# Value and feed-forward loads issued from the ScalarE queue instead of the SyncE queue, in a one-core attention decode kernel

## The chip, the cores and the metric

The kernel runs on one core of a Trainium2 chip. The metric is device time in microseconds (us). The kernel before takes 692.99 us (median of 4 runs, 691.93 to 693.73). A run counts as slow when it is over 1.5% above the fastest run of the same kernel.

In this text K5 is the key load of head 5, V5 its value load, wo1 the second load of output weights (each serves four heads). "Ring" is the line of packets that one issuing engine's loads form at the DMA engines (in the profiles q1 for SyncE, q10 for ScalarE). A "slot" is one half of the double buffer that holds keys or values. "PV" is the product of the softmax probabilities and the values, "fold" the sum of a position's 128 products of key and query.

## The reference, cut to what matters

One token of a transformer block: a layer norm modulated by a condition vector, attention over a cache of 16384 positions in 32 heads of 128, then a gated feed-forward layer.

```python
    B, Sq, D = (1, 1, 640)
    Hq, Hkv, Sk, Dh = (32, 32, 16384, 128)          # bf16 caches: 4 MB of keys and 4 MB of values a head
    ...
    scores = jnp.einsum('bhqd,bhkd->bhqk', q, k) * Dh ** (-0.5)
    p = _softmax(scores, axis=-1)
    o = jnp.einsum('bhqk,bhkd->bhqd', p, v)
    ...
    h = _layernorm(x, axis=-1) * (1 + ca) + sa
    x = x + ga * _A_ref(h, A_k_cache, A_v_cache, A_wq, A_wo)
    h = _layernorm(x, axis=-1) * (1 + cb) + sb
    x = x + gb * _B_ref(h, B_w_gate, B_w_up, B_w_down)
```

There is one query per head, so every byte of the caches is used once: 290 MB have to come in, nearly all of it keys and values.

## The kernel before

The program is a list of operations, each with an engine, a position and the operations that it waits for. Each engine runs its own in order of position; a DMA belongs to the engine that issues it, and that engine stands still until the DMA's waits are met and its issue is done: in the kernel before SyncE waits 556.4 us in all for the first folds that free key slots.

```python
        def lead(h):
            return 1 if h < H - 8 else 2          # keys run ahead of values by 1 head, by 2 in the last 8 heads
        ...
        order = []                                # order of the loads on SyncE's queue
        for h in range(H):
            while nk < min(H, h + lead(h) + 1):
                order.append(("k", nk)); nk += 1  # (two lines joined here)
            if h % G == 0:                        # G = 4
                order.append(("wo", h // G))
            order.append(("v", h))
        ...
            d_k[h] = plan.dma(qpos["k", h], kring[:, s2], ..., deps=[o_fold1[h - 2]] if h >= 2 else [])
            d_wo[g] = plan.dma(qpos["wo", g], woring[:, g % 2],
                               A_wo[...].rearrange("(g p) n -> p g n", p=128), ...)   # rows of 1280 bytes
            vdeps = [o_pvlast[h - 2]] if h >= 2 else [o_mod_a, o_mod_b]
            d_v[h] = [plan.dma(qpos["v", h] + 0.01 * c, vring[...], ..., deps=vdeps) ...]
        ...
            o_mult[h]  = op(DVE,  ..., deps=[d_k[h], o_qbc[h]])          # keys times query
            o_fold1[h] = op(DVE,  ..., deps=[o_mult[h], ...])            # first half of the sum; frees the key slot
            o_fold[h]  = op(PE,   ..., deps=[o_fold1[h], ...])           # rest of the sum
            o_red[h]   = op(DVE,  ...)
            o_max[h]   = op(DVE,  ...)
            o_gm[h]    = op(POOL, ..., deps=[o_max[h]])                  # maximum over partitions
            o_nb[h]    = op(ACT,  ..., deps=[o_gm[h]])
            o_exp[h]   = op(ACT,  ..., deps=[o_nb[h], ...])
            o_pvlast[h] = op(PE,  ..., deps=[o_exp[h], d_v[h][0], ...])  # PV; frees the value slot
        ...
        # after the last head, on SyncE's queue: w_gate, w_up, w_down (three loads, rows of 1280 bytes)
```

(Cuts are marked with dots. The comments are added here.) On PE, PV of head h stands ahead of the fold of head h+1 (of h+2 in the last eight heads), so the heads form one chain.

## Time and profile before

| | before |
|---|---|
| span of the profiled execution | 690.0 us |
| DMA, mean over the span | 422 GB/s |
| one key or value load: 8 packets of 32 KB on each of 16 engines, 1.21 us a packet | 9.7 us |
| multiply of head 0, 25, 30, 31 starts at | 38.1, 526.4, 621.7, 640.0 us |
| from the multiply of head 31 to the end | 50.0 us |

The page's 40 slices of the span (busy tenths of the 16 DMA engines, then GB/s) and its table of DMA queues (packets, MB, time of the packets as a share of 16 engines' span), kernel before:

```profile
DMA  9999999999999999999999999999999999999995
GB/s 385 422 423 435 434 427 428 427 431 429 430 419 433 434 431 434 420 438 426 430 433 425 432 429 428 427 428 429 437 432 421 434 432 427 425 433 424 400 425 202
...
q1 hardware_dynamic: 16368, 290.48, 98.8%
```

Nine tenths or more in all slices but the last, and all of it on queue q1, SyncE's. The DMA engines have no room: q1's packets alone take 98.8% of their time. The chain of waits followed back from the last instruction, by engine and then by line, kernel before:

```profile
DMA 40%; DVE 21%; PE 18%; POOL 18%; ACT 2%; issue 1%; SPq 1%
DMA kring<-in_A_k_cache_dram 36%; POOL gm L417 18%; DVE kring L397 13%; PE psb L407 9%; PE psb L436 7%; DVE f L399 6%; DMA kring<-in_B_w_down_dram 4%; DVE S_sb L411 2%; ACT P_sb L421 1%; PE psb L470 1%; DVE pm L414 1%; SPq L71 1%; PE psb L523 0%; PE psb L388 0%; ACT nb L419 0%
```

Keys are what is waited for most (36%), but over half of the chain is computation: POOL's maximum, the multiply, PE's fold and PV. Two of the groups of instructions (busy us, mean ns; then idle time before them and its cause):

```profile
L397 DVE TENSOR_TENSOR kring<-kring,qbc_sb 128x16384 bf16<-128x16384 bf16 x32 | 278.0, 8687 | 30.2 <-DMA kring<-in_A_k_cache_dram 28.5
L417 POOL PARTITION_ALL_REDUCE gm<-pm x32 | 136.7, 4272 | 333.5 <-DVE pm L414 327.5
```

The maximum takes 0.35 us by itself and 8.73 us when the next head's multiply (8.69 us) has started just ahead of it; 4.27 is a mean of the two kinds. In this execution 15 of the 32 maxima start 0.17 to 0.18 us after a multiply and take 8.71 to 8.73 us; the 17 others start while no multiply runs and take 0.35. Whether a head's maximum or the next head's multiply starts first is a race that decides 8 us.

The same kernel's timeline in time order (start us, duration us, engine), the first loads of values and the first multiply:

```profile
21.37 0.34 SPq L71 DMA_DIRECT2D vring<-in_A_v_cache_dram  x1
...
38.08 8.69 DVE L397 TENSOR_TENSOR kring<-kring,qbc_sb 128x16384 bf16<-128x16384 bf16 x1 [13.97 <-DMA kring<-in_A_k_cache_dram]
...
51.26 0.33 SPq L71 DMA_DIRECT2D kring<-in_A_k_cache_dram  x1
...
51.62 0.43 SPq L71 DMA_DIRECT2D vring<-in_A_v_cache_dram  x1
```

V0 waits for the modulation weights, which lie in its slot, and has K0, K1 and wo0 ahead of it in the ring; K2 and V1 come at 51.

Two stretches of the view by windows (us; busy us and count of PE, weight loads, DVE, ACT, POOL; PE clock; DMA share; GB/s):

```profile
70.00:78.00 8.00, 6.03 (x40) 2.84 (x32) 3.43 (x4) 1.00 (x3) 2.61 (x2) 0.88 1.02 436
78.00:84.00 6.00, 0.00 (x0) 0.00 (x0) 6.00 (x1) 0.00 (x0) 6.00 (x1) 0.56 1.00 431
...
576.00:584.00 8.00, 7.76 (x48) 3.38 (x40) 2.46 (x4) 1.00 (x3) 1.75 (x1) 0.72 1.04 446
584.00:600.00 16.00, 6.20 (x49) 2.52 (x50) 13.04 (x3) 2.42 (x9) 12.36 (x2) 0.68 0.99 426
```

And the end of the timeline, last two multiplies, then the last head's maximum and the first ScalarE step after it:

```profile
621.69 8.68 DVE L397 TENSOR_TENSOR kring<-kring,qbc_sb 128x16384 bf16<-128x16384 bf16 x1
...
639.97 8.68 DVE L397 TENSOR_TENSOR kring<-kring,qbc_sb 128x16384 bf16<-128x16384 bf16 x1
...
659.35 0.35 POOL L417 PARTITION_ALL_REDUCE gm<-pm  x1 [6.00 <-DVE psb L499]
659.74 0.20 ACT L419 ACTIVATE nb<-gm 128x1 f32<-128x1 f32 x1 [5.37 <-POOL gm L417]
```

ScalarE starts 0.04 us after the maximum has ended.

### The profile page before, as it was taken

Reading aid. Unit: us, or ns where it says so; the run is one execution under the profiler, and the core shown is the slowest. Engines: PE = TensorE matmul, PEld = TensorE weight load, DVE = VectorE, ACT = ScalarE, POOL = GpSimd, SP = SyncE. Lnnn points to the kernel's source line nnn. Section 1 sums busy time; section 2 is a strip of 40 time slices with the busy share of each in tenths; the row PEclk is TensorE's granted clock in tenths of the full one; section 3 lists DMA queues with packets and bytes.
Section 4 is the critical chain, followed back from the end, with each engine's and each line's share of the span. In section 5 each row is a group of like instructions: output and inputs, shape, how many; then the busy total and the mean of one; then the engine's idle time right before and its main releaser. Section 6 shows DMA issues by size and latency. Waiting matters only on the chain.

```text
span 690.0 us, 5939 instructions
## 1 busy us (share of the span) xinstructions
PE 305.9 (44%) x2602; PEld 150.5 (22%) x2602; DVE 453.8 (66%) x151; ACT 80.1 (12%) x306; POOL 280.4 (41%) x75
## 2 busy tenths in 40 slices
PE   1503454545444334455432455444335345454464
PEld 1401122222212122222111222212112122221144
DVE  0077767676778876657787566668766676767800
ACT  0100101111111111110111111101011011111110
POOL 0006666565677554000405033304054365667700
PEclk9997666666767666666766666657666666767675
DMA  9999999999999999999999999999999999999995
GB/s 385 422 423 435 434 427 428 427 431 429 430 419 433 434 431 434 420 438 426 430 433 425 432 429 428 427 428 429 437 432 421 434 432 427 425 433 424 400 425 202
DMA packets 16398, 290.86 MB, mean 422 GB/s; under 512 B 1458, under 2 KB 7284, under 8 KB 7284
## 3 DMA queue, kind: packets, MB, share of 16 engines
q1 hardware_dynamic: 16368, 290.48, 98.8%
q8 instruction: 20, 0.33, 0.2%
q14 instruction: 6, 0.05, 0.0%
q10 hardware_dynamic: 4, 0.00, 0.0%
HBM read 290.47 MB, written 0.00 MB: 421 GB/s over the span
## 4 chain that ended last, share of the span: by engine, by line
DMA 40%; DVE 21%; PE 18%; POOL 18%; ACT 2%; issue 1%; SPq 1%
DMA kring<-in_A_k_cache_dram 36%; POOL gm L417 18%; DVE kring L397 13%; PE psb L407 9%; PE psb L436 7%; DVE f L399 6%; DMA kring<-in_B_w_down_dram 4%; DVE S_sb L411 2%; ACT P_sb L421 1%; PE psb L470 1%; DVE pm L414 1%; SPq L71 1%; PE psb L523 0%; PE psb L388 0%; ACT nb L419 0%
## 5 line engine op out<-in xcount | busy, mean ns | idle before, releaser
L397 DVE TENSOR_TENSOR kring<-kring,qbc_sb 128x16384 bf16<-128x16384 bf16 x32 | 278.0, 8687 | 30.2 <-DMA kring<-in_A_k_cache_dram 28.5
L417 POOL PARTITION_ALL_REDUCE gm<-pm x32 | 136.7, 4272 | 333.5 <-DVE pm L414 327.5
L436 PE MATMUL psb<-vring,P_sb 128*32 128x512 bf16 x992 | 108.6, 616 | 138.3 <-DMA vring<-in_A_v_cache_dram 138.3
L424 POOL PARTITION_ALL_REDUCE Ls<-rs x32 | 140.7, 4396 | 27.3 <-ACT P_sb L421 27.3
L407 PE MATMUL psb<-f,ident 128*128 128x512 bf16 x512 | 135.0, 421 | 27.9 <-DVE f L399 27.9
L399 DVE TENSOR_TENSOR f<-kring 128x8192 bf16<-128x8192 bf16 x32 | 141.6, 4425 | 1.1
L411 DVE TENSOR_REDUCE S_sb<-psb 128x128 f32<-128x512 f32 x32 | 22.1, 692 | 153.2 <-PE psb L407 153.2
L470 PE MATMUL psb<-On,woring 128*128 128x1 bf16 x160 | 11.6, 182 | 160.7 <-ACT On L462 159.7
L407 PEld LDWEIGHTS psb<-f,ident 128*128 128x128 bf16 x512 | 50.7, 104 | 120.5 <-DVE f L399 49.5
L436 PEld LDWEIGHTS psb<-vring,P_sb 128*32 128x32 bf16 x992 | 33.5, 138 | 190.8 <-DMA vring<-in_A_v_cache_dram 140.4
L470 PEld LDWEIGHTS psb<-On,woring 128*128 128x128 bf16 x160 | 8.9, 130 | 162.3 <-ACT On L462 162.3
L419 ACT ACTIVATE nb<-gm 128x1 f32<-128x1 f32 x32 | 6.5, 203 | 307.6 <-POOL gm L417 307.6
L447 PEld LDWEIGHTS psb<-sel,acc_sb 128*128 128x128 f32 x248 | 32.3, 191 | 5.8 <-ACT acc_sb L441 1.2
L441 ACT ACTIVATE acc_sb<-psb 128x512 f32<-128x512 f32 x31 | 18.5, 597 | 117.9 <-PE psb L436 117.8
L447 PE MATMUL psb<-sel,acc_sb 128*128 128x1 f32 x248 | 29.4, 240 | 0.7 <-ACT acc_sb L441 0.7
L426 ACT ACTIVATE lnl<-Ls 128x1 f32<-128x1 f32 x32 | 6.4, 201 | 115.8 <-POOL Ls L424 115.8
L388 PE MATMUL psb<-R_sb,ones_bf 128*128 128x128 bf16 x32 | 8.3, 259 | 23.6 <-ACT R_sb L385 23.6
L421 ACT ACTIVATE P_sb<-S_sb,nb 128x128 bf16<-128x128 f32 x32 | 12.8, 401 | 1.0
L385 ACT ACTIVATE R_sb<-ident,q_r 128x128 bf16<-128x128 bf16 x32 | 12.5, 389 | 0.0
L391 ACT ACTIVATE qbc_sb<-psb 128x128 bf16<-128x128 f32 x32 | 8.9, 277 | 11.2 <-PE psb L388 11.2
L414 DVE TENSOR_REDUCE pm<-S_sb 128x1 f32<-128x128 f32 x32 | 9.2, 286 | 1.1
L308 POOL PARTITION_ALL_REDUCE st<-st x2 | 0.8, 391 | 20.8 <-DVE x L488 11.2
(62 smaller groups left out, 80.3 us busy)
## 6 DMA issues: line engine op xcount, KB each, us to landing
kring<-in_A_k_cache_dram SPq DMA_DIRECT2D x32, 4096.0 KB, 25.6
vring<-in_A_v_cache_dram SPq DMA_DIRECT2D x31, 4096.0 KB, 34.4
wreg<-in_A_wq_dram SPq DMA_DIRECT2D x1, 5120.0 KB, 27.1
woring<-in_A_wo_dram SPq DMA_DIRECT2D x8, 640.0 KB, 25.5
vring<-in_w_mod_dram SPq DMA_DIRECT2D x1, 4800.0 KB, 14.3
vring<-in_A_v_cache_dram SPq DMA_DIRECT2D x4, 1024.0 KB, 9.7
wreg<-in_B_w_gate_dram SPq DMA_DIRECT2D x1, 2160.0 KB, 16.7
wreg<-in_B_w_up_dram SPq DMA_DIRECT2D x1, 2160.0 KB, 21.6
```

The costliest lines, as they stand in the source:

```text
L397: o_mult[h] = op(DVE, base, lambda e, kslot=kslot, qb=qb: e.tensor_tensor(out=kslot, in0=kslot, in1=qb, op=ALU.mult), deps=[d_k[h], o_qbc[ ...
L399: o_fold1[h] = op(DVE, base + 8.8, lambda e, kslot=kslot: e.tensor_tensor(out=f1[:], in0=kslot[:, :, 0:64], in1=kslot[:, :, 64:128], op=AL ...
L407: r = e.matmul(S_ps[s2][:].rearrange("p (t r) -> p t r", r=GC), lhsT=ident[:], rhs=f1[:, :, GC * m:GC * (m + 1)], start=(m == 0), stop=(m ...
L411: o_red[h] = op(DVE, base + 17.0, lambda e, s2=s2: e.tensor_reduce(out=S_sb[:, s2], in_=S_ps[s2][:].rearrange("p (t r) -> p t r", r=GC), a ...
L414: o_max[h] = op(DVE, base + 19.3, lambda e, h=h, s2=s2: e.tensor_reduce(out=pm[:, h:h + 1], in_=S_sb[:, s2], axis=AX.X, op=ALU.max), deps= ...
L417: o_gm[h] = op(POOL, base + 19.6, lambda e, h=h: e.partition_all_reduce(gm[:, h:h + 1], pm[:, h:h + 1], channels=128, reduce_op=bass.bass_ ...
L421: o_exp[h] = op(ACT, base + 20.4, lambda e, h=h, s2=s2, sp=sp: e.activation(out=P_sb[:, sp, 0:TT], in_=S_sb[:, s2], func=ACTF.Exp, scale=S ...
L424: o_L[h] = op(POOL, base + 21.0, lambda e, h=h: e.partition_all_reduce(Ls[:, h:h + 1], rs[:, h:h + 1], channels=128, reduce_op=bass.bass_i ...
L436: r = e.matmul(acc_ps[s2][q4:q4 + 32, :], lhsT=P_sb[:, sp, 4 * j:4 * j + 32], rhs=vring[:, s2, 4 * j:4 * j + 4, :].rearrange("p a d -> p ( ...
L441: o_acc[h] = op(ACT, vbase + 9.0, lambda e, s2=s2: e.activation(out=acc_sb[:, s2, :], in_=acc_ps[s2][:], func=ACTF.Copy), deps=[o_pvlast[h ...
L447: r = e.matmul(OT_ps[:, h:h + 1], lhsT=acc_sb[:, s2, 128 * i:128 * (i + 1)], rhs=sel[:, i:i + 1], start=(i == 0), stop=(i == 3))
L470: r = e.matmul(attn_ps[:, cc:cc + 1], lhsT=wv[:, cc, :], rhs=On[:, h:h + 1], start=(h == 0 and cc == 0), stop=(h == H - 1 and cc == KC - 1 ...
```

## The change

Its intent: put values on a second queue, so that a value load need not stand behind a key load whose slot is still in use, and the other way round. Keys and output weights stay on SyncE.

```diff
+        def vpos(h):
+            if h < 2:
+                return 1.97
+            return T0 + (h - 2) * PERIOD + 10.5 + PERIOD * lead(h - 2) + 9.2
 ...
-            d_v[h] = [plan.dma(qpos["v", h] + 0.01 * c, vring[...], ...
-                               ("v", s2) if nvp == 1 else ("vp", s2, c), deps=vdeps, name=...) for c in range(nvp)]
+            d_v[h] = [plan.dma(vpos(h) + 0.01 * c, vring[...], ...
+                               ("v", s2) if nvp == 1 else ("vp", s2, c), deps=vdeps, eng="act", name=...) for c in range(nvp)]
 ...
+        QA = vpos(H - 1) + 0.1
-        d_wg = plan.dma(QE, wg_v, ..., "wg", deps=[o_qmm], name="dma_wg")
+        d_wg = plan.dma(QA, wg_v, ..., "wg", deps=[o_qmm], eng="act", name="dma_wg")
 ... # w_up and the three w_down loads in the same way, behind it
```

More of the change, by code (lines that the diff above doesn't have):

```diff
@@ L381, in build @@
             vdeps = [o_pvlast[h - 2]] if h >= 2 else [o_mod_a, o_mod_b]
-            d_v[h] = [plan.dma(qpos["v", h] + 0.01 * c, vring[:, s2, c * VP:(c + 1) * VP, :], kv(A_v, h)[:, c * VP:(c + 1) * VP, :],
-                               ("v", s2) if nvp == 1 else ("vp", s2, c), deps=vdeps, name="dma_v%d_%d" % (h, c)) for c in range(nvp)]
+            d_v[h] = [plan.dma(vpos(h) + 0.01 * c, vring[:, s2, c * VP:(c + 1) * VP, :], kv(A_v, h)[:, c * VP:(c + 1) * VP, :],
+                               ("v", s2) if nvp == 1 else ("vp", s2, c), deps=vdeps, eng="act", name="dma_v%d_%d" % (h, c)) for c in range(nvp)]
             o_R[h] = op(ACT, base - 15.0 if h > 0 else 2.5, lambda e, h=h, s2=s2: e.activation(
@@ L476, in build @@
         QE = float(len(order)) + 1.0
-        d_wg = plan.dma(QE, wg_v, B_wg.rearrange("(p k) n -> p k n", k=KC), "wg", deps=[o_qmm], name="dma_wg")
-        d_wu = plan.dma(QE + 0.01, wu_v, B_wu.rearrange("(p k) n -> p k n", k=KC), "wu", deps=[o_qmm], name="dma_wu")
+        QA = vpos(H - 1) + 0.1
+        d_wg = plan.dma(QA, wg_v, B_wg.rearrange("(p k) n -> p k n", k=KC), "wg", deps=[o_qmm], eng="act", name="dma_wg")
+        d_wu = plan.dma(QA + 0.01, wu_v, B_wu.rearrange("(p k) n -> p k n", k=KC), "wu", deps=[o_qmm], eng="act", name="dma_wu")
         wd_src = B_wd[0:128 * FJ, :].rearrange("(j p) n -> p j n", p=128)
         NJA = FJ - 3
-        d_wd = [plan.dma(QE + 0.02, wd_v[:, 0:NJA], wd_src[:, 0:NJA], "wd0", deps=[o_fold1[H - 2]], name="dma_wd0"),
-                plan.dma(QE + 0.03, wdr_v[0:FR], B_wd[128 * FJ:F, :], "wdr", deps=[o_fold1[H - 2]], name="dma_wdr"),
-                plan.dma(QE + 0.04, wd_v[:, NJA:FJ], wd_src[:, NJA:FJ], "wd1", deps=[o_fold1[H - 2]], name="dma_wd1")]
+        d_wd = [plan.dma(QA + 0.02, wd_v[:, 0:NJA], wd_src[:, 0:NJA], "wd0", deps=[o_fold1[H - 2]], eng="act", name="dma_wd0"),
+                plan.dma(QA + 0.03, wdr_v[0:FR], B_wd[128 * FJ:F, :], "wdr", deps=[o_fold1[H - 2]], eng="act", name="dma_wdr"),
+                plan.dma(QA + 0.04, wd_v[:, NJA:FJ], wd_src[:, NJA:FJ], "wd1", deps=[o_fold1[H - 2]], eng="act", name="dma_wd1")]
         o_abf = op(ACT, TE, lambda e: e.activation(out=attn_bf[:], in_=attn_ps[:, 0:KC], func=ACTF.Copy), deps=[o_wo[H - 1]], name="attn_bf")
```

## The prediction

(Two sentences are cut from it, about the maximum beside the multiply and about how two rings are served: they told of the hardware what no trace had shown. No term of the sum is cut: 6 + 14 - 3 = 17, with up to 4 for a late K31, taken as 18. That the rings share evenly and bring no bandwidth, on which terms 1 and 2 rest, was the author's assumption at that point; what the traces then showed is in point 1 of "Why the prediction was wrong".)

> **What bounds the kernel now.** The page shows the 16 DMA engines 9 tenths busy or more in all 40 slices but the last, 422 GB/s on average. In the packet records a 32 KB packet takes 1.21 us, so a 4 MB key or value load (8 packets per engine) costs 9.7 us. 64 of them are 623 us; with the weights the engines have about 680 us of work in a span of 690. Issue time is no limit: 0.33 us a load, which lands 25.6 us (keys) or 34.4 us (values) later. What can change is the order in which bytes arrive, and the gaps.
>
> A second limit is close. In the chain of waits, heads 0 to 9 and 25 to 31 run on computation: multiply 8.7, fold 4.4, PE fold 4 to 5, reductions 1.0; the maximum on GpSimd takes 8.73 us when the next head's multiply runs (else 0.35); then exp, PV 3.5. From the multiply of head 25 (526.4) to that of 31 (640.0) a head takes 18.9 us, and the end comes 50 us later, 3 of them waits for feed-forward loads. [...]
>
> **What the change does.** 35 value and 5 feed-forward loads leave SyncE's ring for ScalarE's. ScalarE issues each in about 0.35 us, off the chain. [...] No bandwidth comes, but the keys lose their place:
>
> 1. Start. V0 and V1 issue at about 23.5 us (today V1: 51.6). They share with wq, K0 and K1: K0 lands near 49.5 instead of 38. All slots are full and K2 is loaded by 78; the next slot comes free when fold 1 of head 1 ends, near 82.5. The engines idle about 6 us.
> 2. Middle. Values run as far ahead as their two slots allow. When K25 lands, about 25.5 value loads have gone before it instead of 24: 14 us. Output weights (1280-byte packets, 55 ns) alternate with 32 KB value packets and hold back the keys behind them.
> 3. Heads 24 to 31. Value loads wait on ScalarE behind the next head's exp; the engines idle some 4 and 2 us. The loop of 18.9 us runs on from a K25 about 20 us late.
> 4. End. The feed-forward loads land before they are needed: about 3 us come back.
>
> Sum: 6 + 14 - 3 = 17, with up to 4 for a late K31: 693 + 18.
>
> **Predicted: 711 us**, 8 in 10 between 701 and 720. Faster by over 2%: 0.02; within 2%: 0.27; slower by over 2%: 0.71.
>
> **What would show it.** First multiply near 50 us (now 38.1); a DMA gap of some 6 us near 80; multiply of head 25 near 546; value loads landing about 20 us after issue; the chain in the last 150 us on computation, without a wait for w_down; about 432 GB/s wherever the DMA isn't idle.
>
> **What would make it wrong.** If the rings don't share evenly (keys first), steps 1 and 2 shrink and the time stays near 693. If two rings fill the engines better than one, it is within 2%. If small packets starve the keys longer, it is above 720.

## More of the kernel before

The view of the line that issues all DMAs (count; shortest, median and longest issue in ns; first and last start), kernel before:

```profile
L71 SPq DMA_DIRECT2D vring<-in_A_v_cache_dram x35: 327/432/1386, 21.4 to 655.1; - x35
...
L71 SPq DMA_DIRECT2D kring<-in_B_w_down_dram x3: 438/2161/15974, 657.1 to 659.8; - x3
```

A value load issues in 0.43 us. One of the w_down loads took 16 us to issue; on SyncE only the store of the result stands behind it, issued at 686.82 us, 11 us after this issue has ended (675.79).

## The result, and the profile after

The changed kernel took 726.53 us (720.12 to 735.83, 4 runs); the ratio to the kernel before is 1.045 (95% interval 1.039 to 1.052). In a second round it took 722.78 us (718.75 to 726.24), 1.044. Ratios are the mean time of one kernel's fast runs over that of the other's of the same rounds, so not quite the ratio of the medians quoted. The loss is 31 to 34 us where 18 was predicted, and the time spreads over 2% from run to run where the kernel before spreads over 0.3%.

The seven executions that are not slow lie within 1.1% (718.75 to 726.54). The first profiled execution was the 735.83 us one, slow. So I read a profile of the second round (722.6 us, span 720.6). Its line numbers are a few higher than before (the multiply is L397 before and L402 after). Slices and queues:

```profile
DMA  9999699999999999999999999999999969999980
GB/s 380 433 431 422 246 437 434 423 429 435 433 383 420 432 435 430 425 429 433 433 397 430 425 435 430 425 430 433 433 416 427 400 281 435 425 428 435 414 319 2
...
q1 hardware_dynamic: 9264, 149.62, 49.2%
q10 hardware_dynamic: 7108, 140.86, 45.7%
```

The work is now halved between q1 (keys) and q10 (ScalarE's), and it has holes: at slices 5, 33 and the last two. Not a slower rate: in the packet records a 32 KB packet's median is 1.21 us in both kernels, on both rings, and between the holes GB/s is what it was. The chain:

```profile
DMA 30%; DVE 25%; PE 22%; POOL 16%; ACTq 3%; ACT 2%; issue 1%; SPq 0%; POOLq 0%; DVEq 0%
DMA kring<-in_A_k_cache_dram 30%; POOL gm L422 16%; DVE kring L402 14%; PE psb L412 12%; DVE f L404 7%; PE psb L441 7%; ACTq L71 3%; DVE S_sb L416 2%; ACT P_sb L426 1%; PE psb L475 1%; PE psb L512 1%; DVE pm L419 1%; PE psb L462 1%; PE psb L529 0%; ACT nb L424 0%
```

A new entry is ACTq, ScalarE's queue issuing DMAs, with 3%. The groups:

```profile
L422 POOL PARTITION_ALL_REDUCE gm<-pm x32 | 220.7, 6897 | 324.0 <-DVE pm L419 300.3
L402 DVE TENSOR_TENSOR kring<-kring,qbc_sb 128x16384 bf16<-128x16384 bf16 x32 | 277.9, 8684 | 51.8 <-DMA kring<-in_A_k_cache_dram 51.8
```

The multiply waits 51.8 us for keys where it waited 30.2, and more maxima lose the race (mean 6.9 us). The start:

```profile
24.50 0.36 ACTq L71 DMA_DIRECT2D vring<-in_A_v_cache_dram  x1
24.90 0.45 ACTq L71 DMA_DIRECT2D vring<-in_A_v_cache_dram  x1
...
49.18 8.69 DVE L402 TENSOR_TENSOR kring<-kring,qbc_sb 128x16384 bf16<-128x16384 bf16 x1 [23.68 <-DMA kring<-in_A_k_cache_dram]
```

V0 and V1 go out at 24.5 us and share the engines with K0: the first multiply moves from 38.1 to 49.2. The windows:

```profile
70.00:78.00 8.00, 0.00 (x0) 0.00 (x0) 8.00 (x1) 0.00 (x0) 8.00 (x1) 0.55 0.82 352
78.00:84.00 6.00, 4.51 (x35) 1.46 (x36) 4.57 (x2) 2.27 (x8) 4.00 (x2) 0.50 0.29 79
...
576.00:584.00 8.00, 5.54 (x40) 1.94 (x41) 5.56 (x2) 2.27 (x8) 4.99 (x2) 0.57 0.27 72
584.00:600.00 16.00, 5.96 (x48) 3.12 (x50) 13.74 (x4) 1.41 (x6) 11.86 (x2) 0.68 0.99 426
```

Against 431 and 446 GB/s before, the engines do little in 78 to 84 and 576 to 584 us. The issues and the end of the timeline:

```profile
L71 ACTq DMA_DIRECT2D vring<-in_A_v_cache_dram x35: 334/334/453, 24.5 to 669.5; - x35
...
L71 ACTq DMA_DIRECT2D kring<-in_B_w_down_dram x3: 457/600/21472, 670.9 to 692.9; - x3
...
L71 ACTq DMA_DIRECT2D wreg<-in_B_w_up_dram x1: 453/453/453, 670.5 to 670.5; - x1
```

```profile
644.55 8.68 DVE L402 TENSOR_TENSOR kring<-kring,qbc_sb 128x16384 bf16<-128x16384 bf16 x1
...
668.67 8.69 DVE L402 TENSOR_TENSOR kring<-kring,qbc_sb 128x16384 bf16<-128x16384 bf16 x1 [5.75 <-DMA kring<-in_A_k_cache_dram]
...
670.95 22.60 ACTq L71 DMA_DIRECT2D kring<-in_B_w_down_dram  x3
...
688.31 0.35 POOL L422 PARTITION_ALL_REDUCE gm<-pm  x1 [23.71 <-DVE psb L505]
693.59 0.20 ACT L424 ACTIVATE nb<-gm 128x1 f32<-128x1 f32 x1 [24.83 <-issue]
```

The view by DMA issues tells the w_down loads apart (KB, us from issue to landing):

```profile
kring<-in_B_w_down_dram ACTq DMA_DIRECT2D x1, 1600.0 KB, 29.2
...
kring<-in_B_w_down_dram ACTq DMA_DIRECT2D x1, 80.0 KB, 29.0
```

Value loads issue in 0.33 us. But one w_down load takes 21.5 us to issue, now on ScalarE. It is the second of the three, the 80 KB one (64 rows, issued at 671.44); the large one ahead of it (1280 rows, 670.95) issues in 0.46 us. And the last head's first ScalarE step (nb) starts 4.9 us after its maximum has ended (688.66), when the issues are over (670.95 + 22.60 = 693.55): the idle time before it is put down to "issue". K31's multiply comes 24.1 us after that of head 30 (18.3 before), and from it to the end are 51.9 us.

Sums over the packet records of the two traces, in bins of 1 us: the DMA engines are idle for 10.2 us of the span before and 38.6 after, and busy for 679.8 and 682.1. The 30.6 us of longer span are in these two differences. The idle time is 1.9 us at the very start (2.0 before), 6.9 near 80, 2.3 in the middle, 6.5 near 580, and 20.9 at the end (7.4 at the end before).

### The profile page after: what moved, and what is told of

The parts are those of the page before. It is cut to its first block, busy times and chain, and to the rows that moved or that the text cites. A ratio compares the mean times of both kernels' runs of the same rounds, so it can differ in the third digit from the quotient of the medians.

```text
span 733.9 us, 5939 instructions
## 1 busy us (share of the span) xinstructions
PE 315.9 (43%) x2602; PEld 153.4 (21%) x2602; DVE 453.3 (62%) x151; ACT 79.2 (11%) x306; POOL 305.6 (42%) x75
## 3 DMA queue, kind: packets, MB, share of 16 engines
q1 hardware_dynamic: 9264, 149.62, 48.3%
## 4 chain that ended last, share of the span: by engine, by line
DMA 33%; DVE 28%; PE 21%; POOL 14%; ACT 2%; issue 1%; SPq 0%; POOLq 0%; DVEq 0%
DMA kring<-in_A_k_cache_dram 33%; DVE kring L402 17%; POOL gm L422 14%; PE psb L412 13%; DVE f L404 8%; PE psb L441 6%; DVE S_sb L416 2%; ACT P_sb L426 1%; PE psb L475 1%; PE psb L512 1%; DVE pm L419 1%; PE psb L462 1%; PE psb L529 0%; PE psb L393 0%; ACT nb L424 0%
## 5 line engine op out<-in xcount | busy, mean ns | idle before, releaser
L422 POOL PARTITION_ALL_REDUCE gm<-pm x32 | 178.5, 5579 | 356.1 <-DVE pm L419 329.2
L402 DVE TENSOR_TENSOR kring<-kring,qbc_sb 128x16384 bf16<-128x16384 bf16 x32 | 277.9, 8685 | 66.2 <-DMA kring<-in_A_k_cache_dram 64.8
L412 PE MATMUL psb<-f,ident 128*128 128x512 bf16 x512 | 151.9, 460 | 161.8 <-DVE f L404 161.8
L429 POOL PARTITION_ALL_REDUCE Ls<-rs x32 | 124.0, 3875 | 27.3 <-ACT P_sb L426 27.3
L412 PEld LDWEIGHTS psb<-f,ident 128*128 128x128 bf16 x512 | 54.7, 112 | 265.3 <-DVE f L404 184.0
L441 PE MATMUL psb<-vring,P_sb 128*32 128x512 bf16 x992 | 101.7, 584 | 0.0
L446 ACT ACTIVATE acc_sb<-psb 128x512 f32<-128x512 f32 x31 | 18.3, 590 | 15.9 <-PE psb L441 15.8
L298 PE MATMUL psb<-silu_c,vring 128*128 128x1 bf16 x150 | 6.2, 178 | 7.1 <-DMA vring<-in_w_mod_dram 7.1
```

What stands on the lines that cost most here:

```text
L402: o_mult[h] = op(DVE, base, lambda e, kslot=kslot, qb=qb: e.tensor_tensor(out=kslot, in0=kslot, in1=qb, op=ALU.mult), deps=[d_k[h], o_qbc[ ...
L412: r = e.matmul(S_ps[s2][:].rearrange("p (t r) -> p t r", r=GC), lhsT=ident[:], rhs=f1[:, :, GC * m:GC * (m + 1)], start=(m == 0), stop=(m ...
L422: o_gm[h] = op(POOL, base + 19.6, lambda e, h=h: e.partition_all_reduce(gm[:, h:h + 1], pm[:, h:h + 1], channels=128, reduce_op=bass.bass_ ...
L429: o_L[h] = op(POOL, base + 21.0, lambda e, h=h: e.partition_all_reduce(Ls[:, h:h + 1], rs[:, h:h + 1], channels=128, reduce_op=bass.bass_i ...
L441: r = e.matmul(acc_ps[s2][q4:q4 + 32, :], lhsT=P_sb[:, sp, 4 * j:4 * j + 32], rhs=vring[:, s2, 4 * j:4 * j + 4, :].rearrange("p a d -> p ( ...
L446: o_acc[h] = op(ACT, vbase + 9.0, lambda e, s2=s2: e.activation(out=acc_sb[:, s2, :], in_=acc_ps[s2][:], func=ACTF.Copy), deps=[o_pvlast[h ...
```

## The experiments

All have correct results unless a wrong one is said to be on purpose. Those based on the changed kernel start with a, those on the kernel before with b. "Idle" is the DMA engines' idle time in the profiled execution, read as above (its last figure is that of the last 30 us of the span); "m31" is the start of the last multiply.

| run | median us | ratio to before | first multiply | idle at the start, middle, near 545 to 590, end | head 30 to 31 | m31 to end |
|---|---|---|---|---|---|---|
| before | 693.0 | 1 | 38.1 | 0, 0, 0, 7.4 | 18.3 | 50.0 |
| after_again | 722.8 | 1.044 | 49.2 | 6.9, 2.3, 6.5, 20.9 | 24.1 | 51.9 |
| a_wo_pool | 718.7 | 1.039 | 47.7 | 5.6, 0, 6.8, 20.0 | 19.4 | 57.6 |
| a_no_wo (wrong result) | 712.0 | 1.029 | 47.3 | 4.1, 0.3, 7.0, 20.3 | 18.8 | 57.9 |
| a_wd_sp | 726.3 | 1.049 | 47.7 | 4.1, 6.1, 6.5, 19.0 | 29.7 | 45.3 |
| a_wo_pool_wd_sp | 709.4 | 1.025 | 47.4 | 4.6, 0, 6.3, 11.7 | 19.9 | 47.7 |
| c1_first_two | 704.7 | 1.016 | 37.7 | 0, 0.7, 7.0, 12.2 | 19.8 | 48.3 |
| c2_lead_one | 702.1 | 1.014 | 38.1 | 0, 0.4, 0, 18.0 | 19.2 | 43.6 |
| a_mid_only | 709.2 | 1.025 | 37.8 | 0, 11.7, 8.7, 7.2 | 19.3 | 49.2 |
| a_tail_sp | 715.2 | 1.031 | 47.6 | 5.1, 5.5, 8.0, 7.2 | 18.3 | 49.3 |
| a_tail_only | 712.1 | 1.028 | 38.0 | 0, 0, 8.0, 18.9 | 29.7 | 45.4 |
| a_v01_sp | 718.5 | 1.035 | 38.3 | 0, 8.8, 5.8, 19.2 | 29.7 | 45.5 |

(Gaps of up to 3.3 us in other places are left out. The last digits of the idle times and of the middle columns are those of one execution each; the runs of one kernel spread by some us.)

### Output weights: the same kernel again, without them beside the keys, without them at all

My theory: besides the value loads it is the output weights that hold back the keys. They consist of 32 packets of 1280 bytes per engine; a packet takes 55 ns, but beside a value load on the other ring they wait for value packets of 1.21 us. In the packet records of the repeated profile (us from the span's start, first packet to end of the last of each load):

```
K5   122.9 to 141.7
wo1  142.3 to 155.5     1.8 us of packets, stretched to 13.2 (3.8 in the kernel before)
V5   143.0 to 154.3
K6   153.8 to 168.4     K6 stands behind wo1: 27 us after K5
```

From 144.5 to 152.5, 97 packets of wo1 start and 97 of V5: one for one. In the first profiled execution (the slow one) the five output-weight loads with 84 to 131 value packets beside them take 12.4 to 13.6 us from first to last packet, the three with at most 16 take 3.4 to 3.9; on the one ring of the kernel before all eight take 3.8 to 5.6.

Heads 6, 14 and 22 of that execution, the ones behind wo1, wo3 and wo5, start their multiply 24 to 27 us after the head before; all other steps but the last are 18 to 20.3.

> The changed kernel again, to see its spread and a profile of a second execution. Theory (packets of output weights starve the keys, and a slot that comes free late then leaves the engines idle): 720 to 736 us, with DMA gaps of 5 to 7 us near 80, 205, 370, 535 and 595 us, and the key load behind output weights landing some 30 us after the key before it. Rival (ScalarE's issue or a lower packet rate of two rings costs the time evenly): no gaps at those places in the faster executions.

Measured: 722.78 us. The gaps near 80 and 580 are there, those near 205, 370 and 535 are only 1.5, 0.6 and 0.2 us: they were large in the slow execution and vary from one execution to the next; the expected 5 to 7 us came true for two of the five places.

```diff
-  d_wo[g] = plan.dma(qpos["wo", g], ..., ("wo", g % 2), deps=...)
+  d_wo[g] = plan.dma(qpos["wo", g] if g == 0 else T0 + (h - 3) * PERIOD + 21.05, ...,
+                     ("wo", g % 2) if g else "wo_first", deps=..., eng="sp" if g == 0 else "pool")
```

> Output-weight loads 1 to 7 leave SyncE's ring for GpSimd's; keys and values as in the changed kernel. Theory: a key load no longer stands behind 32 small packets per engine that alternate with value packets, so the key loads after wo1, wo3, wo5 and wo7 land about 11 us sooner, the three gaps of 5 to 6 us near 205, 370 and 535 go, and the tail shortens by about 10: 697 to 705 us. Rival A (values ahead of keys by themselves cost it all, small packets are harmless): 720 to 730. Rival B (ScalarE's in-order issue delays the values): 720 to 730.

Measured: 718.65 us, ratio 1.039: a miss. The mechanism showed (no step between heads over 22 us, no gap in the middle, K31 on time; head 30 starts its multiply 5.0 us sooner), but the time hardly moved. The table says where part of it went: the end after m31 grew from 51.9 to 57.6 us.

```diff
+  if g < 2:
       d_wo[g] = plan.dma(...)
+  else:
+      d_wo[g] = d_wo[g % 2]          # b_no_wo: the same edit of the kernel before
```

> Output-weight loads 2 to 7 left out (heads from 8 on use old weights: wrong result on purpose). Their own packets are 6 x 1.85 = 11 us. Theory: besides those 11 us, the gaps near 370 and 535 and the late K31 go too: 692 to 702 us; the first episode (wo1, gap near 205) stays. Rivals: only the 11 us, 712 to 718.

> The same left out of the kernel before (wrong result on purpose), the control: one ring has nothing to alternate with, so only the packets' own 11 us should go, all theories 681 to 685 us.

Measured: 712.03 and 684.11 us. In the control 7.7 us went, in the changed kernel 10.8, so only 3 us more: the rivals' number, not mine. Here too K31 is on time (18.8) and the end is longer (57.9). In both runs ScalarE's first step of the last head starts late, because it is still issuing w_down: 8.8 us late in a_no_wo. A load that was made earlier only met another wait.

### The w_down issue on ScalarE

```diff
-  d_wd = [plan.dma(QA + 0.02, ..., eng="act", name="dma_wd0"), ...     # three loads
+  d_wd = [plan.dma(QE + 0.02, ..., name="dma_wd0"), ...                # back on SyncE
```

> Only the three w_down loads go back to SyncE's queue, placed after the last key load. New theory of the tail: in the last profile ScalarE spent 21.5 us issuing the first w_down load [...], so the first step of the last head's softmax there began 4.9 us after its input was ready (8.8 us in the run without output weights). Then this run shows no such wait and is 4 to 9 us faster than the changed kernel: 713 to 719. Rival (issue on ScalarE never matters): 720 to 727, with the last head's maximum to exp still 5 us apart.

Measured: 726.28 us: a miss again. (The expectation takes the load that was held for the first of the three; by the view above it is the second, of 64 rows, issued right behind the first.) The wait itself is gone, as the end of its timeline shows (the multiplies of heads 30 and 31, then maximum and nb):

```profile
645.81 8.69 DVE L402 TENSOR_TENSOR kring<-kring,qbc_sb 128x16384 bf16<-128x16384 bf16 x1 [0.32 <-DMA kring<-in_A_k_cache_dram]
...
675.51 8.69 DVE L402 TENSOR_TENSOR kring<-kring,qbc_sb 128x16384 bf16<-128x16384 bf16 x1 [9.19 <-DMA kring<-in_A_k_cache_dram]
...
694.93 0.35 POOL L422 PARTITION_ALL_REDUCE gm<-pm  x1 [26.93 <-DVE psb L505]
695.32 0.20 ACT L424 ACTIVATE nb<-gm 128x1 f32<-128x1 f32 x1 [23.19 <-POOL gm L422]
```

ScalarE starts 0.04 us after the maximum, and m31 to the end is 45.3 us instead of 51.9. But K31 came 29.7 us after K30, held back by wo7 beside V29 in this execution. So each cure alone exposes the other wait. From the multiply of head 30 to the end it is 76.0 us in the repeated changed kernel, 77.0 with output weights moved, 75.0 with w_down moved.

```diff
  # a_wo_pool_wd_sp: both edits above
```

> Output weights on GpSimd's queue and w_down on SyncE's together. Each alone left the tail at 75 to 77 us from the multiply of head 30 to the end: without the small packets K31 came in time (19 us) but ScalarE stood in the w_down issue (end 58 us after the last multiply); with w_down on SyncE the stall went (45 us) but K31 was late (30 us). Theory (two waits in parallel that hide each other): both gone, 19 + 45 = 64, 706 to 711 us. Rival (the engines' remaining bytes set that time): still 75 to 77, 715 to 720.

Measured: 709.38 us, ratio 1.025, inside the expected range:

```profile
637.74 8.69 DVE L402 TENSOR_TENSOR kring<-kring,qbc_sb 128x16384 bf16<-128x16384 bf16 x1 [1.29 <-DMA kring<-in_A_k_cache_dram]
...
657.67 8.68 DVE L402 TENSOR_TENSOR kring<-kring,qbc_sb 128x16384 bf16<-128x16384 bf16 x1
...
676.60 0.35 POOL L422 PARTITION_ALL_REDUCE gm<-pm  x1 [5.55 <-DVE psb L505]
676.98 0.20 ACT L424 ACTIVATE nb<-gm 128x1 f32<-128x1 f32 x1 [4.91 <-POOL gm L422]
```

19.9 + 47.7 = 67.6 us, as in the kernel before (18.3 + 50.0). The two edits gain 13.4 us together (722.8 to 709.4), while one alone gains 4.1 and the other loses 3.5, both within the spread of the changed kernel. The parallel waits at the end are 8.4 us of it (76.0 to 67.6); the rest comes before head 30, where the moved output weights no longer hold back keys. With output weights out of the way, moving w_down is worth 9.3 us (718.65 to 709.38), close to the 8.9 us that nb stands late in the profile of a_wo_pool.

### Is it the small packets?

```diff
-  A_wo[...].rearrange("(g p) n -> p g n", p=128)
+  A_wo[...].rearrange("(p g) n -> p g n", p=128)     # rows of 5120 bytes, a quarter of the packets; permuted: wrong result
```

> The changed kernel with each output-weight load made of 128 packets of 5 KB instead of 512 of 1.25 KB (rows permuted: wrong result on purpose). Theory 1 (one packet each in turn: a value load has only 8 packets per engine, so 8 of output weights go through beside it and the rest at once after it): output weights still take 10 to 13 us when a value load is in flight, keys are as late as before, 719 to 728 us. Theory 2 (small size itself): 710 to 716.

Measured: 727.54 us (one of the four runs, 732.61, is slow), theory 1. With a value load in flight the output weights still take 11.7 to 12 us (wo1: 139.3 to 151.2), without one 2.2 to 3.9 (wo4, wo2, wo6). In the repeated profile wo1, with 32 packets per engine, ended 1.2 us after V5 with its 8 (155.5 and 154.3) and took 13.2 us; with 8 packets per engine it is still 11.9. So the size of the packets, 1.25 or 5 KB, is not what matters here. Fewer than 8 packets an engine were not tried.

> Control: output-weight loads 1 to 7 of the kernel before on GpSimd's queue, keys and values together on SyncE's. All theories: 690 to 694 us, since the engines were never idle; two rings alone don't slow this kernel where nothing important stands behind the small load.

Measured: 693.96 us, ratio 1.002. With keys and values on one ring the move gains nothing, so what it cured in the changed kernel was the sharing.

### The gap near 80 us, and which head wins the race

```diff
-  deps=[d_k[h], o_qbc[h]], name="mult%d" % h)
+  deps=[d_k[h], o_qbc[h], o_gm[h - 1] if h >= 1 else None], name="mult%d" % h)
```

> As the changed kernel, but each head's multiply on VectorE also waits for the maximum (GpSimd) of the head before: 0.35 us instead of 8.7 [...], so exp, PV and the freeing of value slots come some 8 us sooner. Theory (slots that come free late leave the engines idle): the gap near 78 shrinks from 6.9 us to about 2.5 (the value load still stands behind lnl on ScalarE), the gap near 576 shrinks too: 709 to 718 us. Rival (the loop of the computation itself is the limit): 32 x 0.5 = 16 us slower than the changed kernel, 735 or more.

Measured: 741.78 us, ratio 1.071: the rival. The gap near 80 did shrink from 6.9 to about 2 us, as it should if it is a slot that comes free late. But the computation now takes 20.48 us a head, more than two loads:

```profile
314.35 8.69 DVE L402 TENSOR_TENSOR kring<-kring,qbc_sb 128x16384 bf16<-128x16384 bf16 x1 [0.57 <-POOL gm L422]
...
327.56 5.65 PE L412 MATMUL psb<-f,ident 128*128 128x512 bf16 x16 [10.01 <-DVE f L404]
...
334.35 0.35 POOL L422 PARTITION_ALL_REDUCE gm<-pm  x1 [11.06 <-DVE pm L419]
...
334.83 8.69 DVE L402 TENSOR_TENSOR kring<-kring,qbc_sb 128x16384 bf16<-128x16384 bf16 x1 [0.57 <-POOL gm L422]
```

PE's fold takes 5.65 us here, after 10 us in which PE was idle, and 3.64 where it follows on PV:

```profile
658.24 3.64 PE L412 MATMUL psb<-f,ident 128*128 128x512 bf16 x16
```

(This line is from the repeated changed kernel.) In the fold of 5.65 us the matmuls start 0.43 us apart for the first 4 us and 0.22 apart after that, in the fold of 3.64 us all 0.22 apart. The last fold of the repeated changed kernel, after 13.8 us of idle PE, takes 5.28 us, its first matmuls again 0.43 apart. What sets the slow start, and how long an idle stretch brings it, no run shows. With the maximum first, PV comes early and fills no time in front of the fold any more. Ending the race was right for the slots and wrong for PE. Of the 19 us against the repeated changed kernel, 5 are at the end, where ScalarE again stood in the w_down issue (nb 9.5 us late).

```diff
  # a_gm_first_v_early: as above, and up to head 25 the value load is issued ahead of lnl (log of the softmax sum) on ScalarE
+  if lead(h - 2) == 1:
+      return T0 + (h - 2) * PERIOD + 30.15
```

> As a_gm_first, and up to head 25 the value load is issued ahead of lnl on ScalarE, so that it waits for PV alone. Theory: gap near 78 gone altogether (V2 issued near 74), 706 to 715 us. If ScalarE's order in the middle cost much, this would be over 5 us below a_gm_first; I expect 1 to 4.

Measured: 743.05 us, far outside its range. The gap near 80 is gone altogether, as expected, and the time is that of a_gm_first. So ScalarE's order in the middle of the kernel costs nothing that the 20.5 us a head don't hide; for the plain changed kernel it is left untested.

### Start, middle and end by themselves

```diff
  # a_v01_sp: values 0 and 1 back on SyncE's queue, behind the first keys
-  plan.dma(vpos(h) + 0.01 * c, ..., eng="act")
+  plan.dma((qpos["v", h] if h < 2 else vpos(h)) + 0.01 * c, ..., eng="sp" if h < 2 else "act")
```

> As the changed kernel, but the first two value loads stay on SyncE's queue behind the first keys. Theory: first multiply at 38 us again, no gap near 80; values still run ahead later, so only the 6.9 us of the first gap come back: 712 to 719 us. Rival (keys that come late by the 12 us at the start cost all of them): 708 to 711. If the gap only moves to the head where the values have caught up, 719 to 724.

Measured: 718.5 us (711.2 to 719.5), ratio 1.035. The first multiply is back at 38.3 us and the first gap is gone; part of it comes back as a gap of 6.7 us near 440 in the profiled execution.

```diff
  # which values are on ScalarE's queue; the feed-forward loads go with those of the last eight heads
+  on_act = 2 <= h < H - 8      # a_mid_only
+  on_act = h < H - 8           # a_tail_sp
+  on_act = h >= H - 8          # a_tail_only
```

> Only the values of heads 2 to 23 on ScalarE's queue; values 0 and 1, values from 24 on and the feed-forward loads on SyncE's in the order of the kernel before. Theory (the loss sits at the ends: first gap 7 us, gap at the change of lead 6.5, tail 14; the two rings in the middle cost only what is left): 693 to 700 us, no gap over 2 us before the last 30 us except a chance one in the middle. Rival (sharing with the keys costs all along the middle): 705 or more.

> Values 0 to 23 on ScalarE's queue, values from 24 on and the feed-forward loads back on SyncE's in the old order, in which the last two keys stand ahead of the values. Theory: the gap near 576 to 600 (6.5 us) and the 14 us of longer idle DMA at the end go, the first gap (6.9) stays: 699 to 706 us. Rival (tail follows from the late keys of the middle): 715 or more.

> The other half alone: values from 24 on and the feed-forward loads on ScalarE's queue, everything before as in the kernel before. Theory: 20 us of the tail and the change of lead, less what values that start from no advance don't lose: 702 to 714 us. Rival (the tail costs only because keys are late by then): 691 to 696.

Measured: 709.23, 715.23 and 712.13 us. a_tail_only is inside its range: the last eight values and the feed-forward loads alone cost 20 us. Twelve of them are there before head 30 (multiply at 634.1 us instead of 621.7), and K31 is again 29.7 us behind K30; with K31 so late, the w_down issue is over before nb needs ScalarE. With the end on one ring (a_mid_only, a_tail_sp) the end is what it was before: 7.2 us of idle DMA in both. Both still miss their ranges, by 9 us each (one of five runs of a_tail_sp, 724.13, is slow; the profile of a_mid_only is of its longest run, 715.99). One reason is the gap near 545, which I had expected to go. In that order K26 stands ahead of V24, and the records of a_mid_only show K26 and V24 issued together after the fold of head 24 had ended (545.1); with values already ahead there was nothing else to load. The other is the middle, with 11.7 and 5.5 us of gaps behind wo3 and wo5. "The loss sits at the ends" was wrong; the rival's number came true for a_mid_only, and with 715.23 just so for a_tail_sp, though there the end was cured as the theory said.

### Closing the account

```diff
  # c1_first_two: a_wo_pool_wd_sp with values 0 and 1 on SyncE's queue
  # c2_lead_one: the same, and
-  return 1 if h < H - 8 else 2
+  return 1
```

> As a_wo_pool_wd_sp, but value loads 0 and 1 stay on SyncE's queue behind the first keys. Theory: first multiply near 38 us, the gap near 80 (4.6 us) gone: 703 to 706 us. If the gap only comes back later: 708 to 711.

> As c1_first_two, and the last eight heads keep the lead of one head that the others have, so that no value slot waits an extra head at the change. Theory: the gap near 570 (6.3 us) goes as well: 696 to 701 us, the rest being the later end of the last head behind the DMA. If that gap comes from the late keys themselves and not from the change of lead: 703 to 706.

Measured: 704.73 us, inside its range, and 702.05 us, 1 us above. In c2 all gaps before the end are gone, and still 10 us are missing to the kernel before. They are at the end: the DMA engines finish the loads at the same time as before (684.2 us, 683.9 before) and then idle, 18.0 us instead of 7.4. The last multiply starts at 656.6 us instead of 640.0, and from there to the end at least 43.6 us of computation follow. What was still to be loaded at the last multiply fits this: 17.1 MB before (an estimate of 40 us at the 430 GB/s of the busy slices, which hides behind the computation), 12.6 MB in the changed kernel, 10.4 MB in c2. Values that came early were loaded in the place of the last key. This last part is read from one profile each; no run tests it by itself.

## Why the prediction was wrong

Point by point:

1. Bound, direction and the loss of the keys' place were right. The engines were full, the second ring brought no rate (1.21 us for a 32 KB packet on either), and the keys lost their place. The two rings took turns packet by packet: K0 and V0 each take 19 to 21 us from first to last packet, nearly twice the 10.9 of K0 on one ring, and wo1 and V5 alternate one for one (97 packets each in 8 us).
2. The start was right: first multiply 49.2 us (predicted near 50), gap 6.9 us (6).
3. The middle was right in its sum and partly by luck: multiply of head 25 at 548.8 us (546). When K25 landed, 24.9 value loads had come, against 24.0 before; predicted 25.5. So the values' advance was worth some 8 us (0.8 to 0.9 loads of 9.7) and not 14; 2.3 us of gaps and a computation that started 3 us later behind its key made up for most of the rest.
4. The idle time at the change of lead was right: 6.5 us in one gap (4 and 2 predicted), and c2_lead_one shows that the change of lead makes it.
5. "Output weights ... hold back the keys behind them" was said and not counted. This is the first step that failed, a term mis-sized: heads behind wo1, wo3 and wo5 start 5 to 7 us later than the others (10 in other executions), and the late K31 was given "up to 4" where it was 6 to 11. With w_down out of the way, moving the output weights is worth 16.9 us (726.28 to 709.38). The prediction's last line, "If small packets starve the keys longer, it is above 720", named this risk, but no size was worked out for it.
6. The second step that failed is "ScalarE issues each in about 0.35 us, off the chain", with the 3 us said to come back at the end. It holds for values (0.33 us). One w_down load took 21.5 us to issue, ahead of the last head's softmax. The kernel before showed 16 us for one of these loads on SyncE, and I had read only the median. With w_down back on SyncE and the output weights moved, the end after m31 is 2.3 us shorter than before (47.7 against 50.0), so most of the 3 us came back there. The wait is not at the load with the most rows of the three: the one of 1280 rows leaves its engine free after 0.46 us, and a smaller one right behind it is held (64 rows here; 384 rows in the kernel before, after 2.2 us for the 64); w_up, 2160 KB just ahead of the three, issues in 0.45 us here and 0.47 before. In both profiles the hold ended within 0.5 us of the first w_down packet (692.9 and 692.5 us here, 675.8 and 675.4 before), in others up to 10 us apart; what exactly the issuing engine waits for, no run shows.

Terms 5 and 6 together are 13.4 us (a_wo_pool_wd_sp against the repeated changed kernel). What is left then, 709.4 against 692.0, is 17.4 us, close to the 18 of the prediction, though point 3 says that its parts were not all of the predicted size. Of it c1 took back 4.7 (start), c2 another 2.7 (change of lead), and the rest, 10 us, I put down to the values that precede the last keys. One thing stays open: why the changed kernel varies by 1 to 2%. The gaps in the middle, 0 to 12 us in the profiles (18 in the slow execution), go with the race between maximum and multiply behind the late keys, but no run forced that race one way without changing the rest.

None of the versions with a right result beats the kernel before.

## What to carry to other kernels

When the profile shows the DMA engines already full, as here (98.8% of the span), ask what a second queue can still bring: here it brought no bandwidth (a 32 KB packet took 1.21 us on either ring), and the order of arrival came from the turns between the rings (97 packets of wo1 beside 97 of V5). The old order, keys ahead of values by one head and then two, was part of the tuning. Before moving loads to an engine that computes, look at the longest issue of each load and not at the median (21.5 against 0.60 us for w_down here), and at what stands behind it on that engine. If one cure moves the time by nothing, look for a wait in parallel before dropping the theory: here two cures were worth 4 us and nothing alone and 13 us together.
